# Attention prepared two chunks ahead, narrow sums in column halves, and one stream of weight conversions, in an attention and mixture-of-experts kernel

## The chip, the core and the metric

One core of a Trainium2 chip. The metric is the device time of one execution in microseconds; lower is better. Engines: PE (TensorE, matrix products), DVE (VectorE), ACT (ScalarE), POOL (GpSimd), and SP, which here issues the transfers between memory and the core's SBUF. PE writes its results into PSUM, eight banks of 512 columns of fp32; DVE and ACT read them there.

## What is computed

The reference has three stages, one after the other, over 4 batches of 768 tokens, 3072 in all:

```python
for t in range(S):                                  # attention, 8 heads of 48
    cur = einsum('bhd,bhe->bhde', u * k[t], v[t])
    y[t] = einsum('bhd,bhde->bhe', r[t], state + cur)
    state = w[..., None] * state + einsum('bhd,bhe->bhde', k[t], v[t])
x = y                                               # 3072 x 384
h = x @ w_in                                        # first MLP, 384 -> 2048 -> 384
x = (maximum(h, 0) + alpha * minimum(h, 0)) @ w_out
logits = x @ w_gate                                 # second: 8 experts, 384 tokens each
for e in range(8):                                  # greedy assignment by logit
    out[mask[e]] = maximum(x[mask[e]] @ w1[e], 0) @ w2[e]
```

The first MLP's weights arrive as 8-byte numbers and are converted on the core.

## The kernel before, in words

**Attention** runs over 24 chunks of 128 tokens (6 per batch, the four batches in turn). Within a chunk the recurrence is written as matrix products: r and k are scaled by powers of w (RT, KT), pA = K R^T for all pairs of tokens, a mask keeps the earlier tokens, the diagonal gets the sums cs of r u k, and y is the sum of the masked product with v and of the carried state SW with r. State products kv are added to SW (L401) and scaled (L382), for all chunks but the last four, which are the ends of the four batches.

The order of the work on each engine is the order in which the program is written. A *turn* (`turn`, L347) works on chunk i and ends chunk i-1, and prepares chunk i+1. It is a generator with three yields; after each part the main loop (L1256) lets one call of the weight stream pass, four a turn, from turn 2 on. The parts:

1. PE: diagonal sums cc of chunk i, four products of 128 columns by 2 (L360), which the trace counts as eight passes; DVE copies them to cs (L363). DVE: two predicated copies of pA into AT of chunk i-1 (L366). PE: state times r into y (SW, L371). PE: transposes of the scaled k of chunk i+1 into pk (L327). POOL: scaling of k for chunk i+2 (L312). ACT: four scalings of the identity by cs into AT (L378), KT from pk (L333). DVE: RT of chunk i+1 (L319). POOL: scaling of the state (L382).
2. PE: state products kv of chunk i (L389), in alternating column halves; PE: AT times v into y (L396), halves too. DVE: two additions Sn of kv (L401). ACT: four more scalings into AT (L404).
3. POOL: product of RT and KT of chunk i+1 (L339), from which the next turn's cc is made. ACT: ysb from y (L409); SP stores it in `xd`.
4. PE: pA of chunk i (L423), in row halves.

After a turn SP issues the loads of chunk i+4 (L1258). `warm` (L249) issues products without use.

**The weight stream** `load_weights` (L459) goes over 32 pieces, 16 of `w_in` and 16 of `w_out`. For each it issues a load some pieces ahead, and `weight_split` (L435) converts one: ACT makes mk (L443), DVE makes ti in three steps (L446, L448, L450) and tf in a fourth (L453), ACT casts tf to the high part (L456) and POOL subtracts for the low part (L457). It yields after each DVE step and after the last two operations, so a piece is five calls. Pieces 0 to 15 are converted in attention, with ti in PSUM; a second stream converts pieces 16 to 31 in the first group of the MLP, with ti in SBUF, five calls per column block.

**The first MLP** (`mlp`, L569) has seven groups of tokens (512, ..., 256). For each of 16 column blocks f: nine products of layer 1 (L649), ACT and DVE make gh and gl (L653 to L673), and twelve products of layer 2 two blocks behind (L599), for which piece f of `w_out` must be converted. In the second group DVE makes the gate's columns (`gate_columns`, L511) from `wgb`, whose buffer takes the converters' place (L616 to L618). Then come routing and the experts, which the change doesn't touch.

## Time and profile before

| what | us |
|---|---|
| median of 3 runs (lowest, highest) | 846.56 (845.14, 846.89) |
| the profiled execution | 845.94 |
| its span, first to last instruction | 843.9 |
| busy: PE, DVE, ACT, POOL | 801.2, 573.7, 407.8, 283.6 |

The profile is one execution. Busy is the time in which an engine had an instruction running; an engine that isn't busy waits, and the trace says for which instruction of which engine. PE's clock is granted by the chip: 1.00 stands for 2.4 GHz, 0.50 for 1.2 GHz. Attention fills about the first 157 us, the first MLP's first group the next 86.

### The profile page before, as it was taken

To read this page: it belongs to the slowest core of one execution; us is meant where nothing else is said; L and a number is where in the kernel's file an instruction comes from. 1 tells how busy PE (TensorE), PEld (TensorE's weight loads), DVE (VectorE), ACT (ScalarE), POOL (GpSimd) and SP (SyncE) were. 2 spreads that over 40 slices of the span, in tenths; PEclk is the share of its full clock that TensorE was granted. 3 is DMA by queue.
4 is the path that set the end of the run, shared out by engine and by line. 5 is a ranking of instruction groups with operands and counts; after the bars stand their busy time and mean duration, and the time that the engine had idled before them with its cause. 6 is when DMAs were issued, how large, how long until landed. Compare 5 with 4: busy or idle time off the path is not lost.

```text
span 843.9 us, 16328 instructions
## 1 busy us (share of the span) xinstructions
PE 801.2 (95%) x5955; PEld 734.0 (87%) x5955; DVE 573.7 (68%) x1535; ACT 407.8 (48%) x875; POOL 283.6 (34%) x268
## 2 busy tenths in 40 slices
PE   7899899899989999999999999997799999999996
PEld 6788788688879999999999999987799899899996
DVE  4777776589969998998988534576766666664221
ACT  2777676656544444453444445651444343344441
POOL 5566675322200000000000000002576766668661
PEclk8899898999999999999999999999899999999998
DMA  5676754242140020021002001004525523535400
GB/s 164 180 205 192 201 175 137 85 131 90 60 150 1 1 75 1 1 72 51 28 20 75 1 1 57 19 1 142 184 75 184 193 87 135 191 107 181 141 29 31
DMA packets 64584, 81.37 MB, mean 96 GB/s; under 512 B 8048, under 2 KB 55408, under 8 KB 64368
## 3 DMA queue, kind: packets, MB, share of 16 engines
q1 hardware_dynamic: 61008, 70.81, 27.1%
q0 software_dynamic: 3072, 9.44, 3.2%
q8 instruction: 49, 0.80, 0.4%
q14 instruction: 39, 0.32, 0.1%
q10 hardware_dynamic: 416, 0.00, 0.0%
HBM read 66.07 MB, written 14.16 MB: 95 GB/s over the span
## 4 chain that ended last, share of the span: by engine, by line
PE 66%; DVE 6%; issue 4%; ACT 2%; POOL 2%; DMA 1%; POOLq 0%; ACTq 0%; DVEq 0%
PE m L599 23%; PE ph L649 20%; PE eph L1099 10%; PE o L1116 9%; PE cnt L789 2%; PE ept L1083 1%; DMA wgb<-in_moe_w_gate_dram 1%; ACT nt L653 1%; DVE gh L662 1%; DVE gt L662 1%; POOL out_dram L1125 1%; POOL wbl L1063 1%; DVE G L784 0%; ACT wbh L456 0%; PE ip L878 0%
## 5 line engine op out<-in xcount | busy, mean ns | idle before, releaser
L649 PE MATMUL ph<-xh,wah 128*128 128x512 f32 (+1 forms) x336 | 122.6, 365 | 0.3 <-ACT gh L654 0.2
L649 PE MATMUL ph<-xl,wah 128*128 128x512 f32 (+1 forms) x336 | 122.4, 364 | 0.3 <-DVE xl L507 0.3
L649 PE MATMUL ph<-xh,wal 128*128 128x512 f32 (+1 forms) x336 | 122.1, 364 | 0.0
L599 PE MATMUL m<-wbh,gl 128*128 128x384 f32 (+1 forms) x352 | 119.4, 339 | 2.5 <-DVE gl L673 2.5
L599 PE MATMUL m<-wbh,gh 128*128 128x384 f32 (+1 forms) x352 | 119.5, 340 | 2.3 <-ACT wbh L456 2.3
L599 PE MATMUL m<-wbl,gh 128*128 128x384 f32 (+1 forms) x352 | 120.4, 342 | 1.3 <-POOL wbl L457 1.3
L653 ACT ACTIVATE nt<-ph 128x512 f32<-128x512 f32 (+1 forms) x112 | 60.2, 537 | 111.2 <-PE ph L649 103.0
L739 POOL COPY L<-M 128x176 f32<-128x176 f32 (+1 forms) x2 | 0.7, 358 | 332.5 <-DVE M L605 311.5
L670 ACT CAST gh<-gt 128x512 fp32r<-128x512 f32 (+1 forms) x96 | 56.3, 587 | 89.4 <-DVE gt L662 89.4
L662 DVE SCALAR_TENSOR_TENSOR gt<-nt,al,gt 128x512 f32<-128x512 f32 (+1 forms) x96 | 67.7, 705 | 45.0 <-ACT gt L654 44.5
L1107 DVE SCALAR_TENSOR_TENSOR hl<-eph,hh 128x384 fp32r<-128x384 f32 x64 | 35.6, 556 | 77.0 <-ACT hh L1102 77.0
L1102 ACT ACTIVATE hh<-eph 128x384 fp32r<-128x384 f32 x64 | 31.5, 492 | 114.5 <-PE eph L1099 111.8
L521 DVE SCALAR_TENSOR_TENSOR junk<-wt,wgb 128x384 f32<-128x384 f32 x128 | 71.3, 557 | 9.1 <-DMA wgb<-in_moe_w_gate_dram 5.2
L599 PEld LDWEIGHTS m<-wbl,gh 128*128 128x128 f32 x352 | 66.2, 188 | 7.7 <-POOL wbl L457 4.4
L649 PEld LDWEIGHTS ph<-xh,wal 128*128 128x128 f32 x336 | 63.4, 189 | 10.9
L599 PEld LDWEIGHTS m<-wbh,gh 128*128 128x128 f32 x352 | 66.2, 188 | 6.2 <-ACT wbh L456 2.7
L649 PEld LDWEIGHTS ph<-xh,wah 128*128 128x128 f32 x336 | 63.4, 189 | 8.6 <-ACT gh L654 0.5
L649 PEld LDWEIGHTS ph<-xl,wah 128*128 128x128 f32 x336 | 63.5, 189 | 8.3 <-DVE xl L507 0.6
L673 DVE TENSOR_TENSOR gl<-gt,gh 128x512 fp32r<-128x512 f32 (+1 forms) x96 | 61.6, 642 | 12.0 <-ACT gh L670 11.9
L1063 POOL TENSOR_TENSOR wal<-raw,wah 128x768 fp32r<-128x768 f32 x32 | 58.4, 1845 | 32.9 <-ACT wah L1062 31.4
L1063 POOL TENSOR_TENSOR wbl<-raw,wbh 128x768 fp32r<-128x768 f32 x32 | 58.6, 1849 | 30.4 <-ACT wbh L1062 30.3
L599 PEld LDWEIGHTS m<-wbh,gl 128*128 128x128 f32 x352 | 66.3, 188 | 2.9 <-DVE gl L673 2.9
(251 smaller groups left out, 1833.6 us busy)
## 6 DMA issues: line engine op xcount, KB each, us to landing
raw<-in_moe_w_dram SPq DMA_DIRECT2D x64, 384.0 KB, 4.7
stg<-in_moe_w_in_dram SPq DMA_DIRECT2D x16, 384.0 KB, 4.4
stg<-in_moe_w_out_dram SPq DMA_DIRECT2D x16, 384.0 KB, 3.1
raw_r<-in_rt_dram SPq DMA_DIRECT2D x24, 224.0 KB, 4.2
raw_k<-in_kc_dram SPq DMA_DIRECT2D x24, 192.0 KB, 4.0
raw_v<-in_vc_dram SPq DMA_DIRECT2D x24, 192.0 KB, 4.2
xd<-ysb SPq DMA_DIRECT2D x48, 96.0 KB, 2.2
md<-raw SPq DMA_DIRECT2D x22, 192.0 KB, 2.0
```

Of the source, the lines that this page charges most:

```text
L521: v.scalar_tensor_tensor(junk, t, 1.0, self.wgb[:, e], op0=ALU.mult, op1=ALU.mult, accum_out=wc[:, f, e:e + 1])
L599: nc.tensor.matmul(acc[t][:, :N], a[:, o], self.wb[b][:, f, :N], start=(f == 0 and n == 0), stop=(f == NF - 1 and n == 2))
L649: nc.tensor.matmul(ph[:, :T], self.wa[a][:, k, fs], b[:, k, :T], start=(n == 0), stop=(n == 8))
L653: nc.scalar.activation(nt[:, :T], ph[:, :T], AF.Relu, scale=-1.0)
L662: v.scalar_tensor_tensor(gt[:, :T], nt[:, :T], self.al[:, f:f + 1], gt[:, :T], op0=ALU.mult, op1=ALU.add)
L670: nc.scalar.copy(h, g)
L673: v.tensor_sub(l, g, h.bitcast(F32))
L1063: self.nc.gpsimd.tensor_sub(to[1], d, to[0].bitcast(F32))
L1099: self.nc.tensor.matmul(ph, w1[a][:, k, f * P:(f + 1) * P], x[b][:, k], start=(n == 0), stop=(n == 8))
L1102: self.nc.scalar.activation(hh, ph, AF.Relu)
L1107: self.nc.vector.scalar_tensor_tensor(hl, ph, 0.0, hh.bitcast(F32), op0=ALU.max, op1=ALU.subtract)
L1116: self.nc.tensor.matmul(self.acc[q], h[a][:, o], w2[b][:, f], start=(f == 0 and n == 0), stop=(f == NS - 1 and n == 2))
```

## The change

Attention prepares chunk i+2 in turn i (LOOK) and needs the deeper buffers for that. The sums of chunk i+1 are made in part 2 of turn i (`sums`), ahead of kv, in eight products of 64 columns; they lie in the last eight columns of the tile that also takes kv (`kvc`). The two weight streams become one, whose loads use the buffers `raw`; what attention doesn't get to is converted in the first MLP group. Four chunks and three weight pieces are loaded ahead of the set-up's branch.

```diff
-EARLY = 16
-WAHEAD = 2
-EARLYC = 2
+WAHEAD = 3
+EARLYC = 4
-NRAW = {"k": 4, "r": 4, "v": 6, "p": 3}
-AHEAD = 4
+NRAW = {"k": 4, "r": 4, "v": 6, "p": 5}
+AHEAD = 5
+LOOK = 2
...
-        self.load_chunk(0)
+        for i in range(EARLYC):
+            self.load_chunk(i)
+            if i:
+                next(self.wl)
...
+        self.kvc = self.pa.tile([P, 4 * D + H], F32, tag="kv", name="kvc")
...
+    def sums(self, i):
+        if i >= NCH:
+            return
+        cc, prod = self.kvc[:, 4 * D:], self.prod.pop(i)
+        for j in range(4):
+            for c in range(2):
+                o = slice(64 * c, 64 * c + 64)
+                self.nc.tensor.matmul(cc[o, 2 * j:2 * j + 2], prod[:, j, o], self.uw[:, j, :], start=True, stop=True,
+                                      skip_group_check=True)
+        cs = self.cs[i] = self.wk.tile([P, H], F32, name="cs")
+        self.nc.vector.tensor_copy(cs, cc)
...
-        RT = self.RT[i] = self.wk.tile([112, 4, P], F32, name="RT", bufs=3)
+        RT = self.RT[i] = self.wk.tile([112, 4, P], F32, name="RT", bufs=4)
...
-        KT = self.KT[i] = self.wk.tile([112, 4, P], F32, name="KT")
+        KT = self.KT[i] = self.wk.tile([112, 4, P], F32, name="KT", bufs=3)
...
-            cc = self.pa.tile([P, H], F32, tag="cc", name="cc")
-            prod = self.prod.pop(i)
-            for j in range(4):
-                nc.tensor.matmul(cc[:, 2 * j:2 * j + 2], prod[:, j, :], self.uw[:, j, :], start=True, stop=True,
-                                 skip_group_check=True)
-            cs = self.wk.tile([P, H], F32, name="cs")
-            v.tensor_copy(cs, cc)
+            cs = self.cs.pop(i)
...
-            y = self.pa.tile([112, 4, P], F32, tag="y", name="y")
+            y = self.pa.tile([112, 4, P], F32, tag="y", bufs=2, name="y")
...
-        self.turn_k(i + 1)
-        self.scale_k(i + 2)
+        self.turn_k(i + LOOK)
+        self.scale_k(i + LOOK + 1)
         if cur:
-            AT = self.AT[i] = self.wk.tile([P, 2, 4, P], F32, name="AT", bufs=3)
+            AT = self.AT[i] = self.wk.tile([P, 2, 4, P], F32, name="AT", bufs=2)
...
-        self.keep_k(i + 1)
-        self.scale_r(i + 1)
+        self.keep_k(i + LOOK)
+        self.scale_r(i + LOOK)
...
         yield
+        self.sums(i + 1)
         kv = None
         if cur and c < NCB - 1:
-            kv = self.pa.tile([112, 4, D], F32, tag="kv", name="kv")
+            kv = self.kvc[:112, :4 * D].rearrange("p (j d) -> p j d", j=4)
...
-        self.product(i + 1)
+        self.product(i + LOOK)
...
     def weight_load(self, shape, src):
+        t = self.rw.tile([P, 2 * DM], F32, name="raw")
...
             ti = (self.pa.tile([P, n], U32, tag="ti", name="ti") if self.pa is not None else
-                  self.stg.tile([P, n], U32, name="ti", bufs=1))
+                  self.pc.tile([P, n], U32, tag="cnt", name="ti"))
...
-        side = self.load_weights(EARLY, 2 * NF)
+        side = self.wl
...
+        K.rw = ctx.enter_context(tc.tile_pool(name="rw", bufs=4, reuse_waits="tile"))
+        wl = K.wl = K.load_weights(WAHEAD)
         K.att_setup(c2)
-        wl = K.load_weights(0, EARLY, WAHEAD)
-        K.scale_k(0, tc.nc.vector)
-        K.scale_k(1)
-        K.prepare(0)
-        drain(cut(wl, WAHEAD))
+        v = tc.nc.vector
+        for i in range(LOOK + 1):
+            K.scale_k(i, None if i else v)
+        for i in range(LOOK):
+            K.scale_r(i)
+            K.turn_k(i)
+            K.keep_k(i)
+            K.product(i, None if i else v)
+        K.sums(0)
+        for i in range(EARLYC, AHEAD):
+            K.load_chunk(i)
         for i in range(NCH + 1):
             merge((K.turn(i), 1), (cut(wl, PACE) if i > 1 else None, 1))
             K.load_chunk(i + AHEAD)
...
-        drain(wl)
+        while K.splitting:
+            next(wl)
         K.warm(4)
```

The product, ysb and set-up tiles get three buffers in the same way. The pool `stg` keeps only the converters' own tiles.

## Rows read from the trace of the kernel before

**Rows 1.** The page: busy time, share of the span and instructions of PE, PEld, DVE, ACT, POOL.

```profile
PE 801.2 (95%) x5955; PEld 734.0 (87%) x5955; DVE 573.7 (68%) x1535; ACT 407.8 (48%) x875; POOL 283.6 (34%) x268
```

**Rows 2.** Table by stretch: us, busy PE, PEld, DVE, ACT, POOL, clock, DMA share, GB/s.

```profile
34.00:130.00 96.00, 88.60 (x1082) 79.32 (x1080) 69.99 (x149) 68.04 (x188) 62.45 (x61) 0.89 0.68 196
...
157.00:243.00 86.00, 79.51 (x373) 67.31 (x373) 69.20 (x119) 49.12 (x96) 18.77 (x16) 0.98 0.37 118
```

**Rows 3.** Timeline of PE in one turn: start, us, engine, line, operation, idle before.

```profile
81.21 1.16 PE L423 MATMUL pA<-RT,KT 48*128 48x128 f32 x16
82.30 1.05 PE L360 MATMUL cc<-uw,prod 112*128 112x2 f32 x8
83.21 1.11 PE L371 MATMUL y<-RT,SW 112*112 112x128 f32 x8
...
84.69 0.61 PE L389 MATMUL kv<-raw_v,raw_p 128*64 128x48 f32 x15
...
85.13 0.22 PE L389 MATMUL kv<-raw_v,raw_p 128*64 128x48 f32 x1
...
86.17 1.16 PE L423 MATMUL pA<-RT,KT 48*128 48x128 f32 x16
```

**Rows 4.** Timeline of PE: pA of chunk 3 and of chunk 19.

```profile
33.31 1.16 PE L423 MATMUL pA<-RT,KT 48*128 48x128 f32 x16
...
129.49 1.16 PE L423 MATMUL pA<-RT,KT 48*128 48x128 f32 x16
```

**Rows 5.** List of waits, 13 to 157 us: waiter, releaser, total us, times, longest.

```profile
PE cc L360 <- POOL prod L339: 12.3, 13, 2.0
```

**Rows 6.** Two waits of cc (timeline of PE), and the clock after them (table by stretch).

```profile
72.37 1.05 PE L360 MATMUL cc<-uw,prod 112*128 112x2 f32 x8 [0.48 <-POOL prod L339]
...
93.46 1.05 PE L360 MATMUL cc<-uw,prod 112*128 112x2 f32 x8 [0.89 <-POOL prod L339]
...
71.20:74.50 3.30, 2.82 (x33) 2.63 (x30) 1.04 (x3) 1.29 (x4) 2.10 (x3) 1.00 0.47 112
...
95.00:98.40 3.40, 3.40 (x36) 3.06 (x35) 2.54 (x6) 2.64 (x9) 0.94 (x1) 0.50 0.68 206
```

**Rows 7.** Timeline of DVE in one turn.

```profile
115.61 1.35 DVE L366 COPY_PREDICATED AT<-later,pA 128x512 f32<-128x512 int32 x2
...
117.45 0.55 DVE L446 TENSOR_SCALAR ti<-stg 128x384 uint32<-128x384 uint32 x1
117.90 0.71 DVE L401 TENSOR_TENSOR Sn<-kv,SW 48x192 f32<-48x192 f32 x2
118.65 0.56 DVE L448 SCALAR_TENSOR_TENSOR ti<-stg,ti 128x384 uint32<-128x384 uint32 x1
...
119.91 0.55 DVE L453 SCALAR_TENSOR_TENSOR tf<-mk,ti 128x384 f32<-128x384 f32 x1
```

**Rows 8.** Timeline of DVE, ACT and PE where attention ends and the MLP begins.

```profile
154.46 1.34 DVE L366 COPY_PREDICATED AT<-later,pA 128x512 f32<-128x512 int32 x2 [2.32 <-PE pA L423]
...
157.50 1.66 ACT L506 CAST xh<-xr 128x512 fp32r<-128x512 f32 x3
...
158.17 0.49 PE L649 MATMUL ph<-xh,wah 128*128 128x512 f32 x1
```

**Rows 9.** The chain of waits in the first MLP group and the start of the second.

```profile
161.17 0.60 ACT nt L653
...
168.79 2.87 PE m L599 x11
...
233.65 6.26 DMA wgb<-in_moe_w_gate_dram
...
247.14 2.08 PE m L599 x12
...
251.32 2.09 PE m L599 x12
```

**Rows 10.** Groups by line, DVE, 160 to 235 us: busy, mean ns, idle before.

```profile
L453 DVE SCALAR_TENSOR_TENSOR tf<-mk,ti 128x384 f32<-128x384 f32 x16 | 17.5, 1094 | 2.5 <-ACT mk L443 2.3
```

More of the change, by code (lines that the diff above doesn't have):

```diff
@@ L169, in att_setup @@
                 self.raw[n, i] = t
-        self.load_chunk(0)
+        for i in range(EARLYC):
+            self.load_chunk(i)
+            if i:
+                next(self.wl)
         self.wk = ctx.enter_context(tc.tile_pool(name="wk", bufs=2))
-        self.stg = ctx.enter_context(tc.tile_pool(name="stg", bufs=WAHEAD + 1))
-        TR = ap.tile([112, 4, P], F32, name="TR")
-        TK = ap.tile([112, 4, P], F32, name="TK")
+        self.stg = ctx.enter_context(tc.tile_pool(name="stg", bufs=2))
+        TR = self.wk.tile([112, 4, P], F32, tag="ysb", bufs=3, name="TR")
+        TK = self.wk.tile([112, 4, P], F32, tag="prod", bufs=3, name="TK")
         PW = ap.tile([112, 8, 4], F32, name="PW")
@@ L216, in att_setup @@
         self.WC = PW[:, 7, :].unsqueeze(2).to_broadcast([112, 4, 112])
-        self.AT, self.prod, self.RT, self.KT = {}, {}, {}, {}
-        for i in range(1, EARLYC):
-            self.load_chunk(i)
+        self.AT, self.prod, self.RT, self.KT, self.cs = {}, {}, {}, {}, {}
+        self.kvc = self.pa.tile([P, 4 * D + H], F32, tag="kv", name="kvc")
         self.branch(fl)
-        for i in range(EARLYC, AHEAD):
-            self.load_chunk(i)
         self.warm(WARM[2])
@@ L244, in range_test @@
         v.tensor_copy(ok, oki)
-        po = self.pa.tile([1, 4], F32, tag="cc", name="pok")
+        po = self.pa.tile([1, 4], F32, tag="y", bufs=2, name="pok")
         nc.tensor.matmul(po, self.ones[:112], ok, start=True, stop=True)
@@ L260, in recurrence @@
         TB = 4
-        St = self.wk.tile([P, 12, D], F32, tag="AT", bufs=3, name="slow_s")
+        St = self.wk.tile([P, 12, D], F32, tag="AT", bufs=2, name="slow_s")
         v.memset(St, 0.0)
@@ L270, in recurrence @@
         with tc.For_i(0, S, TB) as t0:
-            rk = self.wk.tile([P, 2, TB, 12], F32, tag="prod", name="slow_rk")
-            vt = self.wk.tile([P, TB, D], F32, tag="AT", bufs=3, name="slow_v")
+            rk = self.wk.tile([P, 2, TB, 12], F32, tag="prod", bufs=3, name="slow_rk")
+            vt = self.wk.tile([P, TB, D], F32, tag="AT", bufs=2, name="slow_v")
             for bh in range(B * H):
@@ L279, in recurrence @@
                     nc.sync.dma_start(vt[4 * bh + g:4 * bh + g + 1], self.v[b, h:h + 1, bass.ds(t0, TB), :])
[L280 removed]
+            py = self.pa.tile([D, TB, 32], F32, tag="y", bufs=2, name="slow_py")
             for t in range(TB):
                 sh = [P, 12, D]
[L283 removed]
+                kv = self.wk.tile(sh, F32, tag="RT", bufs=4, name="slow_kv")
                 v.tensor_tensor(kv, rk[:, 1, t].unsqueeze(2).to_broadcast(sh),
                                 vt[:, t].unsqueeze(1).to_broadcast(sh), op=ALU.mult)
[L286 removed]
+                z = self.wk.tile(sh, F32, tag="KT", bufs=3, name="slow_z")
                 v.tensor_tensor(z, kv, wu[:, 1].unsqueeze(2).to_broadcast(sh), op=ALU.mult)
@@ L289, in recurrence @@
                 v.tensor_tensor(z, z, rk[:, 0, t].unsqueeze(2).to_broadcast(sh), op=ALU.mult)
-                yp = self.wk.tile([P, D], F32, tag="ysb", name="slow_yp")
+                yp = self.wk.tile([P, D], F32, tag="ysb", bufs=3, name="slow_yp")
                 v.tensor_reduce(yp, z.rearrange("p j e -> p e j"), axis=AX, op=ALU.add)
@@ L331, in keep_k, with product @@
             return
-        KT = self.KT[i] = self.wk.tile([112, 4, P], F32, name="KT")
+        KT = self.KT[i] = self.wk.tile([112, 4, P], F32, name="KT", bufs=3)
         self.nc.scalar.copy(KT, self.pk)
-    def product(self, i):
+    def product(self, i, g=None):
         if i >= NCH:
             return
-        t = self.prod[i] = self.wk.tile([112, 4, P], F32, name="prod")
-        self.nc.gpsimd.tensor_mul(t, self.RT[i], self.KT[i])
-    def prepare(self, i):
-        self.scale_r(i)
-        self.turn_k(i)
-        self.keep_k(i)
-        self.product(i)
+        t = self.prod[i] = self.wk.tile([112, 4, P], F32, name="prod", bufs=3)
+        (g or self.nc.gpsimd).tensor_mul(t, self.RT[i], self.KT[i])
     def turn(self, i):
@@ L405, in turn @@
         yield
-        self.product(i + 1)
+        self.product(i + LOOK)
         if prev:
-            ysb = self.wk.tile([112, 4, P], F32, name="ysb")
+            ysb = self.wk.tile([112, 4, P], F32, name="ysb", bufs=3)
             nc.scalar.copy(ysb, y)
@@ L426, in weight_load @@
     def weight_load(self, shape, src):
+        t = self.rw.tile([P, 2 * DM], F32, name="raw")
+        n = shape[1] * shape[2]
         if src.dtype == F32:
-            t = self.stg.tile(shape, F32, tag="stg", name="stg")
+            t = t[:, :n].rearrange("p (a b) -> p a b", a=shape[1])
             self.nc.sync.dma_start(t, src)
         else:
-            t = self.stg.tile([P, shape[1] * shape[2], 2], U32, tag="stg", name="stg")
+            t = t.bitcast(U32)[:, :2 * n].rearrange("p (n w) -> p n w", w=2)
             self.nc.sync.dma_start(t.rearrange("p (a b) w -> p a (b w)", a=shape[1]), src)
@@ L457, in weight_split, with load_weights @@
         nc.gpsimd.tensor_sub(dst_l, t, dst_h.bitcast(F32))
-    def load_weights(self, n0, n1, ahead=1):
+    def load_weights(self, ahead):
+        n0, n1 = 0, 2 * NF
+        self.split_done = 0
         d = 2 if self.w_in.dtype != F32 else 1
```

9 lines of the change are left out of this document (4 added, 5 removed).

## The prediction

> **What bounds the kernel now.** I read the page first: TensorE (PE) is busy for 95% of the span [rows 1], so what counts is where PE waits or runs at half rate. A table by stretch comes next: in the attention turns from 34 to 130 us PE is 88.6 of 96 us busy, but at a mean granted clock of 0.89; its two levels are 2.4 and 1.2 GHz, so some 22% of that stretch, 21 us, ran at 1.2 [rows 2]. Then the timeline of one clean turn: from one pA to the next 4.96 us, of which the diagonal sums cc take 0.91 (82.30 to 83.21), SW and pk 1.48, kv 0.44 (84.69 to its last matmul at 85.13), y 1.04, pA 1.09 [rows 3]. Yet the sixteen turns from pA of chunk 3 to pA of chunk 19 take 96.2 us, 6.01 each [rows 4]. The list of waits names the first cause: cc waits for POOL's product, 13 times, 12.3 us [rows 5]. The product needs KT, KT comes on ScalarE (ACT) behind four AT scalings, and those need the cs of the turn before: a ring through four engines about as long as a turn. The second cause follows from it. Where the wait was 0.48 (cc at 72.37) the clock stayed at 1.00; where it was 0.89 (cc at 93.46), with 0.91 of narrow cc behind it, the next 3.4 us were granted 0.50 [rows 6].
>
> VectorE (DVE) is the engine next in line. Per turn: the two predicated copies and RT 1.84 (115.61 to 117.45), a conversion step 0.45 to 0.63 (117.45 to 117.90; two from 118.65 to 119.91 in 1.26), 0.58 taken, Sn 0.75 [rows 7].
>
> **The change, part by part.** *Looking two chunks ahead.* KT, RT and the product are made a turn earlier, and cs too, so the ring is cut: cc no longer waits for POOL, and the AT scalings no longer wait for cs. POOL has the same four operations as before with a turn more of slack, and the deeper buffers (RT, KT, product, ysb, y) cover it. The second y bank frees PE from the ysb copy, which no row shows as a wait. AT goes from three buffers to two: AT(i) then needs y of turn i-1 finished, which ACT waits for anyway with its ysb copy just ahead; nothing. Chunk loads are issued five ahead instead of four but are used a chunk earlier, so SP has the same lead.
>
> *Sums in column halves.* Eight passes of 128 columns become sixteen of 64. The kv row is the like of it: sixteen passes of 64 and 48 columns in alternating halves, 0.44 [rows 3]. I take 0.44 between 0.40 and 0.91 (halves one after the other). A clean turn of PE becomes 4.96 - 0.91 + 0.44 = 4.49. The Trainium skill (TensorE: Matmul & The Clock Gate, Part 3, "What overlaps and what doesn't") says that a weight load overlaps running matmuls only where the row group differs; the halves share all rows, so by it the sums would stay at 0.91. The kv row speaks against that, its halves sharing all rows too; by the rule the sum below would be some 2 us higher, in the four last turns.
>
> *The shared bank: a new wait.* cc and kv now lie in one tile. Program order is: PE writes the sums, DVE copies them to cs, PE writes kv, DVE adds Sn. Every PSUM tile of the kernel before fills a bank of its own and goes strictly from all of PE's writes to the reader, so no row shows PE writing one part of a tile while DVE reads another. Either the wait is by address (kv does not wait, cost 0) or for the whole bank (kv waits for cs). I take the bank, nearest to the strict alternation of kv and Sn now. The Trainium skill (PSUM — Partial Sum Buffer, "PSUM bank collisions raise a hardware error") has this as its rule, guard by bank and not by address; no row here shows it.
>
> With that wait PE holds kv, and behind it y and pA, until DVE reaches cs. DVE in the turn: copies and RT 1.84, one conversion step 0.58, cs 0.17; a hand-over 0.1 (ACT's first cast ends 0.12 before the first MLP matmul [rows 8]); PE then kv, y, pA 2.57; hand-over 0.1: 5.36 from pair of copies to pair of copies. DVE itself: 1.84 + 0.58 + 0.17 + 0.7 until kv has landed + Sn 0.75 + three steps 1.74 = 5.78. The stream has five calls a piece, four with a DVE step, and four calls a turn; so in five turns one has all four steps (5.8), three miss one behind Sn (5.4), one misses the one ahead of cs (about 5.2): mean 5.45. PE stands 0.96 a turn, 1.3 in the long one.
> Sixteen turns: 16 x (5.45 - 6.01) = **-9.0**. Turns 2 and 3, which ran clean before, go from 4.96 to 5.45: **+1.0**.
>
> *Clock in attention.* Wait and narrow sums together are now 0.96 + 0.44 = 1.40 in most turns, like 0.48 + 0.91 = 1.39 at 72 us, where the clock stayed; in the long turn 1.35 + 0.44 = 1.79, like 0.89 + 0.91 = 1.80 at 93 us, where it fell [rows 6]. One turn in five of sixteen is three falls, at half rate for 3.4 us each, 1.7 lost: **+5**. Ends: 0, and one in every other turn, +14.
>
> *The last four chunks* have no kv, so nothing waits for cs. PE: 4.49 - 0.44, say 4.1 a turn; 16.4, plus pA and hand-over 1.3 to the last pair of copies: 17.7. Before, from 129.49 to 154.46, 24.97 with a wait and a half-rate stretch [rows 4, 8]: **-7.3**. DVE needs 3.8 there.
>
> *One stream of conversions.* Three of its calls lie in the set-up; 92 calls in 23 turns and three more convert 19 pieces before the MLP, 16 before this. The three more lie in turns 21 to 24, which have room on DVE, but five steps stand behind the last pair of copies: 1.24 + 5 x 0.58 = 4.15, and a cast of 0.5 on ACT, ahead of the first xh cast, which came 3.04 after the copies began (154.46 to 157.50) [rows 8]: **+1.5**. Three weight loads are now queued on SP among the first chunks; SP issues, it doesn't compute, and the first pA waits for POOL's second product, so I book nothing, with 2 us either way.
> In the first MLP group the first layer-2 batch waited for its converted weights until 168.79, and batch 17 starts at 247.14; the batches then follow each other in 4.18 (247.14 to 251.32) [rows 9]. After: pieces 0 to 2 of w_out are ready, so batch 0 starts after three layer-1 batches (158.17 to 161.17, then twice 2.1) and 0.4 for gl: 165.8. DVE then has 13 groups with five calls, and its last conversion step takes 1.09 there with both inputs in SBUF [rows 10] against 0.55 in attention with one in PSUM [rows 7]; with ti moved to PSUM a group needs 0.67 + 2.4 + 0.65 = 3.7 of DVE, under PE's 4.18. The stream ends three groups earlier, so wgb, whose buffer waits for the converters' space and which held the chain for 6.26 us [rows 9], lands in time. Batch 17 at 165.8 + 17 x 4.18 = 236.9: **-10.2**. From there PE is the bound as before.
>
> Sum: +1.0 - 9.0 + 5 - 7.3 + 1.5 - 10.2 = -19.0. The profiled execution took 845.94 (span 843.9, 2.0 around it); 845.9 - 19.0 = 826.9, and the median of the runs stands 0.6 above the profiled one: **827**.
>
> **Rivals.** *No bank wait.* If kv waits by address, a turn is the larger of PE's 4.49 and DVE's 1.84 + 0.1 + 0.75 + 3.2 x 0.58 = 4.55; say 4.6 with jitter: 16 x (4.6 - 6.01) = -22.6, the early turns -1, no falls. -1 - 22.6 - 7.3 + 1.5 - 10.2 = -39.6: 807. For it: the sums and kv touch different columns of the tile. Against: the strict alternation in every bank now. Chance 0.12.
> *The MLP keeps its pace.* If DVE still sets the first group's pace, or wgb still comes late, the gain is only the first wait: from 168.79 to 165.8 and what was lost to a half-rate stretch after it, some 5 of the 10.2: 832. For it: DVE is 69 of 86 us busy there now [rows 2]; against: the 3.7 above. Chance 0.10.
> *Slower: the new wait brings the clock down.* It stands in each of the 16 turns, between sums and kv, and both neighbours are narrow. If most turns fall to half rate as at 93 us, each costs 1.7; the other terms are worth 24, so it decides from the fourteenth fall on. Sixteen: 846.5 - 24 + 27 = 849.5. For it: a wait of 0.89 was enough once; against: the cc that stood behind it is halved. Chance 0.05.
> *The change doesn't do what it says*: product(i) might still be late, as POOL's scaling waits for raw_k. Two turns of lead cover that; I give it none.
>
> **How the numbers follow.** Forecast 0.73, at 827, its own range 816 to 839 (clock 0 to +14, turn length 0.2 x 16, start 2). About a tenth, all of the address case, lies below 811, and a tenth above 839 with the clock. So 811 to 839. A measurement of this kernel tells 0.2%, 1.7 us, from no change. Faster 0.94, same 0.01, slower 0.05.
>
> **What would show it.** Right: PE's wait for POOL's product gone; a wait of kv for DVE's cs in turns 1 to 19 with 0.8 to 1.3 each; pA to pA 5.4; sums in 0.44; layer-2 batch 0 right behind the third layer-1 batch; no DVE wait for wgb; xh later behind the last copies by 1.5. Wrong: kv straight behind the sums (then 807), a clock under 0.85 from 34 to 125 us, or batches of the first group at 4.3 and more.

## The result, and the profile after

The changed kernel takes 836.03 us (median of 7 runs, 834.65 to 841.36); the kernel before, on the same chip, 846.56. The ratio is 0.9888, with a 95% interval of 0.9862 to 0.9914: faster by 1.1%, and inside the range, but by 10.5 us where 19.5 were forecast. The profiled execution took 834.65, its span is 832.9 us, 11.0 less than before. These 11.0 fall on the stretches of the sum as follows:

| stretch | forecast, us | measured, us |
|---|---|---|
| start to pA of chunk 3 (33.31, now 38.19) | +1.0 | +4.9 |
| sixteen turns to pA of chunk 19 (96.18, now 86.73) | -9.0, and +5 for the clock | -9.5 |
| to pA of chunk 23 (23.71, now 15.42), forecast to the copies behind it | -7.3 | -8.3 |
| to the first ph (4.97, now 6.63) | +1.5 | +1.7 |
| first ph to layer-2 batch 17 (88.97, now 89.05) | -10.2 | +0.1 |

The page of the changed kernel, busy time by engine, as [rows 1]:

```profile
PE 785.5 (94%) x6147; PEld 717.9 (86%) x6147; DVE 576.9 (69%) x1536; ACT 406.7 (49%) x875; POOL 280.2 (34%) x269
```

The table by stretch, with the columns of [rows 2]; the first line is exactly the sixteen turns:

```profile
38.20:124.90 86.70, 74.34 (x1209) 65.56 (x1208) 70.83 (x149) 66.97 (x185) 61.94 (x61) 1.00 0.74 215
147.00:236.00 89.00, 82.98 (x385) 69.79 (x386) 69.99 (x124) 47.38 (x92) 19.52 (x22) 0.98 0.29 93
```

The clock of the turns went from 0.89 to 1.00, and PE is now idle for 12 of 86.7 us: it was slow, now it waits. What for, the list of waits from 13 to 157 us says, which had POOL's product at this place [rows 5]:

```profile
PE kvc L390 <- DVE cs L318: 15.3, 20, 2.0
```

One turn on PE, as [rows 3]. From pA to pA it is 5.25 to 5.33; every fifth takes 5.85; the mean of the sixteen is 86.73 / 16 = 5.42, for which 5.45 was forecast:

```profile
70.96 1.16 PE L424 MATMUL pA<-RT,KT 48*128 48x128 f32 x16
72.06 1.13 PE L371 MATMUL y<-RT,SW 112*112 112x128 f32 x8
73.02 0.60 PE L339 MATMUL pk<-ident,raw_p 128*112 128x128 f32 x4
73.55 0.63 PE L315 MATMUL kvc<-uw,prod 112*64 112x2 f32 x16
74.75 0.61 PE L390 MATMUL kvc<-raw_v,raw_p 128*64 128x48 f32 x15 [0.56 <-DVE cs L318]
...
76.23 1.16 PE L424 MATMUL pA<-RT,KT 48*128 48x128 f32 x16
```

The sums and kv write different columns of one tile, and kv stands 0.56 us for the copy cs. Why the copy is late, DVE's timeline shows: a conversion step stands ahead of it, and Sn behind it then waits 0.84 for kv.

```profile
74.07 0.56 DVE L453 SCALAR_TENSOR_TENSOR ti<-raw,ti 128x384 uint32<-128x384 uint32 x1
74.53 0.16 DVE L318 COPY cs<-kvc 128x8 f32<-128x8 f32 x1
75.53 0.72 DVE L402 TENSOR_TENSOR Sn<-kvc,SW 48x192 f32<-48x192 f32 x2 [0.84 <-PE kvc L390]
```

Where the first MLP group begins, the timelines of POOL and DVE show something new. POOL's memsets of a routing constant, which ran from 150.1 to 155.4 beside the end of attention before, now run beside the group's start, and two small DVE instructions take over 4 us; the first gt waits behind them:

```profile
148.12 5.24 POOL L139 MEMSET ohr<- 128x3072 bf16 x2
...
149.15 4.30 DVE L120 TENSOR_SCALAR tri<-jp 128x128 bf16<-128x128 int32 x1
149.28 4.18 DVE L133 TENSOR_SCALAR io<-io 128x32 f32<-128x32 f32 x1
...
153.82 0.74 DVE L669 SCALAR_TENSOR_TENSOR gt<-nt,al,gt 128x512 f32<-128x512 f32 x1
```

Within the group, ACT and DVE in one column block:

```profile
166.22 0.51 ACT L459 CAST wbh<-tf 128x384 fp32r<-128x384 f32 x1 [1.28 <-DVE tf L456]
166.64 0.59 ACT L660 ACTIVATE nt<-ph 128x512 f32<-128x512 f32 x1
167.13 0.59 ACT L661 ACTIVATE gt<-ph 128x512 f32<-128x512 f32 x1
...
165.63 0.55 DVE L456 SCALAR_TENSOR_TENSOR tf<-mk,ti 128x384 f32<-128x384 f32 x1
166.10 0.69 DVE L680 TENSOR_TENSOR gl<-gt,gh 128x512 fp32r<-128x512 f32 x1
167.75 0.75 DVE L669 SCALAR_TENSOR_TENSOR gt<-nt,al,gt 128x512 f32<-128x512 f32 x1 [0.96 <-ACT gt L661]
```

Read it as a ring. The stream's five calls now fill one block exactly, so a piece's cast (its fifth call) is the last thing that ACT is given in a block, and it waits for tf, the fourth DVE step. The next block's nt and gt stand behind that cast, though ph has long been there, and DVE's L669 waits 0.96 us for gt. DVE goes idle for the very engine that waits for DVE. The block takes 4.67 us (163.08, 167.75, 172.42), where PE needs 4.2. At 4.3 and more the prediction had called itself wrong. In the kernel before the stream's first call in this group was a load alone, and the cast fell behind gh of the following block.

At the start, ACT's first AT scaling was at 14.98 before; now it waits for SP, which leaves the branch (L229, around the recurrence, whose tiles share AT's buffers) only at 18.5:

```profile
18.57 1.28 ACT L378 ACTIVATE AT<-ident,cs 128x128 f32<-128x128 f32 x4 [4.80 <-SPq L229]
```

### The profile page after: what moved, and what is told of

It is laid out like the page before. It is cut to its first block, busy times and chain, and to the rows that moved or that the text cites. A ratio compares the mean times of both kernels' runs of the same rounds, so it can differ in the third digit from the quotient of the medians.

```text
span 832.9 us, 16734 instructions
## 1 busy us (share of the span) xinstructions
PE 785.5 (94%) x6147; PEld 717.9 (86%) x6147; DVE 576.9 (69%) x1536; ACT 406.7 (49%) x875; POOL 280.2 (34%) x269
## 3 DMA queue, kind: packets, MB, share of 16 engines
q1 hardware_dynamic: 61008, 70.81, 27.5%
## 4 chain that ended last, share of the span: by engine, by line
PE 69%; DVE 15%; issue 6%; ACT 4%; POOL 2%; DMA 1%; DVEq 0%; POOLq 0%; SPq 0%; ACTq 0%
PE m L605 21%; PE ph L656 19%; PE eph L1106 10%; PE o L1123 9%; PE cnt L796 2%; DVE AT L366 2%; DVE ti L451 2%; DVE ti L449 2%; PE y L397 2%; PE kvc L390 1%; DVE ti L453 1%; DVE tf L456 1%; PE pA L424 1%; DVE RT L331 1%; ACT nt L660 1%
## 5 line engine op out<-in xcount | busy, mean ns | idle before, releaser
L669 DVE SCALAR_TENSOR_TENSOR gt<-nt,al,gt 128x512 f32<-128x512 f32 (+1 forms) x96 | 67.8, 706 | 52.7 <-ACT gt L661 52.7
L1114 DVE SCALAR_TENSOR_TENSOR hl<-eph,hh 128x384 fp32r<-128x384 f32 x64 | 35.6, 557 | 77.4 <-ACT hh L1109 77.4
```

The costliest lines, as they stand in the source:

```text
L669: v.scalar_tensor_tensor(gt[:, :T], nt[:, :T], self.al[:, f:f + 1], gt[:, :T], op0=ALU.mult, op1=ALU.add)
L1114: self.nc.vector.scalar_tensor_tensor(hl, ph, 0.0, hh.bitcast(F32), op0=ALU.max, op1=ALU.subtract)
```

## The experiments

Each is an edit of the changed kernel and computes all of it. What stands against the kernel before is a ratio. The chips differ: in five groups of runs the kernel before took 846.4, 845.7, 855.8, 852.2 and 846.0 us. Its start also varies from run to run. So most readings are by stage, from one trace of each:

| kernel | ratio (95%) | pA of chunk 3 | 16 turns | to first ph | first ph to the group's stores | rest |
|---|---|---|---|---|---|---|
| before | 1 | 33.3 | 96.2 | 28.7 | 79.3 | 606.4 |
| changed | 0.989 (0.986, 0.991) | 38.2 | 86.7 | 22.0 | 82.2 | 603.7 |
| e1_phase | 0.981 (0.978, 0.984) | 38.5 | 86.7 | 22.0 | 75.1 | 604.0 |
| e2_consts | 0.989 (0.986, 0.992) | 40.8 | 90.4 | 22.4 | 80.5 | 604.2 |
| e3_loads | 0.987 (0.984, 0.990) | 35.7 | 86.7 | 22.0 | 82.2 | 603.6 |
| e4_sums_first | 0.995 (0.992, 0.997) | 36.2 | 88.3 | 27.6 | 82.3 | 603.6 |
| e5_full | 0.992 (0.988, 0.995) | 39.1 | 86.7 | 23.0 | 82.3 | 603.6 |
| e6_warm | 0.990 (0.985, 0.994) | 37.0 | 90.9 | 22.0 | 82.2 | 603.7 |
| e8_sums_before_step | 0.987 (0.983, 0.992) | 36.6 | 83.8 | 22.4 | 82.3 | 603.6 |
| e9_sums_mid | 0.977 (0.971, 0.982) | 35.6 | 78.8 | 25.6 | 82.2 | 611.4 |
| e10_mid_prod | 0.975 (0.972, 0.978) | 34.9 | 76.4 | 22.9 | 82.2 | 603.8 |
| e11_prod_up | 0.988 (0.982, 0.994) | 37.5 | 90.8 | 22.0 | 82.3 | 610.3 |
| e12_phase_mid | 0.964 (0.960, 0.968) | 36.1 | 76.4 | 22.9 | 75.2 | 611.5 |
| e14_all | 0.964 (0.960, 0.969) | 37.1 | 77.3 | 22.9 | 72.6 | 611.1 |
| e15_loads_warm | 0.984 (0.980, 0.989) | 38.2 | 89.1 | 22.0 | 82.2 | 608.1 |
| e16_all_warm | 0.962 (0.959, 0.965) | 36.0 | 76.7 | 22.9 | 72.6 | 609.5 |
| e17_chunks | 0.990 (0.985, 0.995) | 38.8 | 86.7 | 22.0 | 82.3 | 608.8 |
| e18_chunk4_first | 0.986 (0.982, 0.990) | 33.8 | 86.7 | 22.0 | 82.2 | 603.8 |
| e19_all_chunk4 | 0.960 (0.957, 0.964) | 31.6 | 78.0 | 22.9 | 74.1 | 603.6 |

The second column from the right is the first MLP group up to the store of its results, 6.8 us before batch 17 in the changed kernel. In the kernel before the group lost more behind its stores, at the wait for wgb. The last column shows which rows share a chip's pace: the only edited thing in it is the routing constants, which four of the kernels make there, and e2_consts shows no more than 0.2 us for them (604.2 against the 604.0 of e1_phase on the same chip).

### The first MLP group

**e1_phase** shifts the stream by one call:

```diff
-                drain(cut(side, rate))
+                drain(cut(side, rate - (gi == 0 and f == 0)))
```

> The stream of weight conversions is drained with four steps instead of five in the first block of the first MLP group and with five from then on, as in the kernel before, so that a piece's cast on ACT comes after the next block's gh and no longer stands, waiting for DVE's tf, ahead of the next block's nt and gt. Theory (the ring of ACT and DVE through the aligned stream holds the group): the block period falls from 4.67 to 4.2 to 4.4 us, DVE's waits of 0.96 for ACT's gt go from most blocks, the m batch that stood at 236.0 comes 4 to 6 us earlier, the whole 830 to 832 us. Rival 1 (DVE's own work, some 4.2 us in a block, and PE's half clock at the group's start hold it): under 1 us, 835 to 836. Rival 2 (the last pieces of w_out are now late for layer two or the gate columns, as one step is left over): 837 or more.

Measured 828.44 us, less than the 830 to 832 expected; the group is 7.1 us shorter, attention unchanged. ACT and DVE after the shift:

```profile
166.16 0.51 ACT L459 CAST wbh<-tf 128x384 fp32r<-128x384 f32 x1
166.57 0.55 ACT L446 ACTIVATE mk<-raw 128x384 f32<-128x384 f32 x1
167.02 0.58 ACT L660 ACTIVATE nt<-ph 128x512 f32<-128x512 f32 x1
...
167.87 0.69 DVE L680 TENSOR_TENSOR gl<-gt,gh 128x512 fp32r<-128x512 f32 x1
168.47 0.75 DVE L669 SCALAR_TENSOR_TENSOR gt<-nt,al,gt 128x512 f32<-128x512 f32 x1
169.13 0.55 DVE L449 TENSOR_SCALAR ti<-raw 128x384 uint32<-128x384 uint32 x1
```

No wait stands in brackets any more: the cast follows gh, and L669 follows gl at once. DVE's block is 3.62 us (164.85, 168.47, 172.09), as the prediction had worked out 3.7, and PE sets the pace. In the chain of waits batches alternate with layer 1 without a gap from the first on, where the chain of the changed kernel had run through ACT and DVE until batch 12 at 215.1:

```profile
157.79 2.02 PE m L605 x10
159.81 2.10 PE ph L656 x9
161.91 2.08 PE m L605 x12
...
229.15 2.12 PE m L605 x12
```

From first ph (147.22) to batch 17 (229.15) it is 81.9 instead of 89.05, where the prediction's terms give 78.8 (88.97 less 10.2). The ring is shown; it cost 7.1 us.

**e2_consts** moves `route_consts` from the start of the first group to block 2 of the second.

> The routing constants (GpSimd's two memsets of 2.65 us and iotas, VectorE's five small instructions) are made in block 2 of the second group instead of at the start of the first. Theory (the memsets run beside VectorE's first steps of the group and stretch its two small instructions from about 0.2 to 4.2 us): the first gt comes 1 to 1.5 us earlier than 153.8, the whole 834.5 to 835. Rival 1 (those instructions overlap work that waits for the first ph anyway, and the stream sets the pace): within 0.4 us of the changed kernel. Rival 2 (in the second group the same instructions stretch too, and layer one waits there): slower by 1 to 3 us.

The group is 1.7 us shorter, and L120 took 0.22 us at its new place. The whole, at 837.11, shows nothing: in this trace the half clock held until 50 us, and the first ph came 6.6 us later. So the effect is read from the stage. With the shifted stream, e14_all takes 72.6 there against 75.2 in e12_phase_mid, 2.5 us less, but not all of that is the constants: e12_phase_mid has a half clock at the group's start (136.5 to 139.8), e14_all has 1.00 throughout. e19_all_chunk4, also without the constants, has a half clock of about that length (134.0 to 137.4) and takes 74.1. So, from one trace of each, 1.1 us of the 2.5 go with the constants and 1.4 with the clock; whether the memsets have a part in the clock is open, since e2_consts has the half clock without them. The changed kernel has it too (147.1 to 150.4). From first ph to batch 17 the steps are 89.05, 81.9 without the ring, 80.9 without the constants too (e19_all_chunk4), and 79.5 without the half clock (e14_all), close to the 78.8 of the prediction.

### The turn

**e8_sums_before_step** issues the sums before the turn's first yield, so that DVE's copy no longer stands behind a conversion:

```diff
+        self.sums(i + 1)
         yield
-        self.sums(i + 1)
```

> The sums and their copy are issued ahead of the turn's first conversion step instead of behind it; TensorE's order stays as it is, only VectorE's copy now comes before the conversion. Theory (kv waits 0.56 us because the copy stands behind a conversion of 0.56, the bank itself costs no more than the copy's way, 0.2 us): kv waits 0.2 us, turns 4.9 to 5.1 instead of 5.27, the long ones 5.5, the whole 830 to 833 us. Rival 1 (VectorE's work sets the turn): turns 5.2 to 5.3, the whole 835 to 836.5. Rival 2 (with shorter turns GpSimd's product comes late for the sums and the clock falls in every fifth turn): long turns of 7 us or more, the whole 836 or more.

By stage, as the theory had it: kv waits 0.27 in the clean turns, which take 4.97; of every five, one takes 5.32 and one 5.38; the sixteen take 83.8 us, of which one early turn of 6.63 holds a half clock (40.5 to 43.8). The whole, 833.97 us, is not clear of the changed kernel: the intervals of the ratios overlap.

```profile
72.64 0.61 PE L390 MATMUL kvc<-raw_v,raw_p 128*64 128x48 f32 x15 [0.27 <-DVE cs L318]
74.13 1.16 PE L424 MATMUL pA<-RT,KT 48*128 48x128 f32 x16
```

**e4_sums_first** goes further: sums at the top of the turn, the copy between the two predicated copies.

```diff
             for q in range(2):
                 v.copy_predicated(...)
+                if q == 0:
+                    self.sums(i + 1)
```

> The sums of the next chunk stand at the top of a turn on TensorE, ahead of the state products and the transposes, and their copy on VectorE between the two predicated copies instead of behind the conversions, so that the products into the bank that sums and kv share come long after the copy. Theory (the wait of 0.56 to 1.1 us for the copy, and VectorE's 0.84 for kv behind it, set the turn): a turn falls from 5.42 to about 4.8 us (then ACT's 4.8 us of work in a turn and TensorE's 4.7 set it), 20 turns, the whole 823 to 827 us. Rival 1 (the work of VectorE and ACT sets the turn, the wait fills a gap): turns 5.2 to 5.4, the whole 832 to 836. Rival 2 (the second predicated copy and the AT behind it are now late for y): turns 5.5 or more, the whole 838 or more.

A miss. The clean turns are 4.63, and yet the whole is 840.78: one turn in five takes long, three of them 8.3 to 9.7. PE's timeline and the table by stretch there:

```profile
66.78 1.16 PE L427 MATMUL pA<-RT,KT 48*128 48x128 f32 x16
69.97 1.02 PE L315 MATMUL kvc<-uw,prod 112*64 112x2 f32 x16 [2.03 <-POOL prod L351]
...
72.00:74.00 2.00, 2.00 (x14) 1.66 (x15) 0.95 (x2) 0.08 (x1) 0.93 (x1) 0.50 0.90 309
```

This is the picture of the kernel before [rows 5, 6]: sums at the top of a turn meet a product that isn't ready, and the half clock follows. POOL's product stood behind the weight subtraction, which waits for ACT's cast:

```profile
67.70 1.00 POOL L463 TENSOR_TENSOR wal<-tf,wah 128x384 fp32r<-128x384 f32 x1 [1.75 <-ACT wah L462]
68.66 1.26 POOL L351 TENSOR_TENSOR prod<-RT,KT 112x512 f32<-112x512 f32 x1
```

**e10_mid_prod** puts the sums between state products and transposes and issues the product at the end of part 1, ahead of that subtraction:

```diff
+        self.sums(i + 1)
         self.turn_k(i + LOOK)
...
+        self.product(i + LOOK)
         yield
-        self.sums(i + 1)
...
-        self.product(i + LOOK)
```

> The sums stand between the state products and the transposes, their copy on VectorE behind the predicated copies, and GpSimd's product two chunks ahead is issued at the end of the turn's first part, ahead of a weight subtraction that it stood behind in some turns. Theory (the copy and kv no longer wait, as the experiment with the sums first showed with clean turns of 4.63; that one lost its gain to a wait of 2.03 us for GpSimd's product in every fifth turn, behind which the clock fell; here the product comes before the subtraction): clean turns 4.6 to 4.8, the long ones under 5.6, no half clock between 40 and 140 us, the whole 822 to 828 us. Rival 1 (another engine, ACT with 4.8 us of work in a turn or GpSimd with 4.2, makes TensorE wait all the same, and the clock falls again): long turns of 7 us or more, the whole 834 to 842.

Measured 824.53 us, with every turn from chunk 3 to chunk 19 at 4.77 to 4.79. PE is busy 75.01 of 76 us at full clock:

```profile
35.00:111.00 76.00, 75.01 (x1205) 65.36 (x1207) 71.08 (x147) 64.82 (x183) 62.42 (x62) 1.00 0.83 242
```

**e9_sums_mid** and **e11_prod_up** each make one half of this edit.

> Half of the edit that gave turns of 4.78: the sums stand between the state products and the transposes, but GpSimd's product stays in the turn's third part, behind the weight subtraction in some turns. Theory (the sums then come before the late product: in the experiment with the sums first the wait was 2.03 us, here 1.1 us of state products lie ahead of them): in every fifth turn TensorE waits 0.5 to 1.2 us for the product, and the half clock comes back, long turns of 6 to 9 us, the whole 830 to 840 us. Rival (the place of the sums alone gives the gain): turns of 4.8 throughout, the whole 822 to 827.

> The other half: GpSimd's product is issued at the end of the turn's first part, the sums stay at the changed kernel's place. Theory (kv still waits for the copy behind a conversion): turns 5.27, the long ones 5.3 to 5.85, the whole 832 to 836 us. Rival (the late product sets the changed kernel's turn too): turns of 5 us or less, the whole 823 to 830.

In the sixteen turns the sums' place brings most of it (78.8), with a wait of 0.97 for the product in every fifth, which then takes 5.82. The half clock that was expected behind that wait came once in three: behind the waits at 67.74 and 92.67 the clock stayed at 1.00, behind the third, in the turn after chunk 19, it fell.

```profile
117.62 0.63 PE L315 MATMUL kvc<-uw,prod 112*64 112x2 f32 x16 [0.98 <-POOL prod L351]
...
119.00:121.50 2.50, 2.50 (x24) 2.17 (x23) 1.65 (x4) 2.41 (x7) 1.68 (x2) 0.50 0.57 205
```

So from pA of chunk 3 to the first ph (108.8 us in the changed kernel, 104.4 here, 99.4 in e10_mid_prod) the sums' place brings 4.4 us and the product's place behind it another 5.0. The product's place alone brings nothing to the clean turns (5.25 to 5.32); its 90.8 holds a half clock in the first turns (43.2 to 53.4).

**e5_full** makes the sums with four full-width products again.

```diff
-            for c in range(2):
-                o = slice(64 * c, 64 * c + 64)
-                self.nc.tensor.matmul(cc[o, 2 * j:2 * j + 2], prod[:, j, o], self.uw[:, j, :], start=True, stop=True,
+            self.nc.tensor.matmul(cc[:, 2 * j:2 * j + 2], prod[:, j, :], self.uw[:, j, :], start=True, stop=True,
```

> The sums are made by four products of 128 columns of the array instead of eight of 64 (as in the kernel before, but into the shared bank and at the changed kernel's place). Theory (the halves save what the two rows show, 1.05 for the eight full products of both trace groups against 0.63 for sixteen halves, some 0.4 us in a turn, and it all lies ahead of the copy that kv waits for): turns 5.27 to 5.5 to 5.7, the last four 3.6 to 4.0, the whole 841 to 846 us. Rival 1 (the copy stands behind a conversion on VectorE anyway, which ends 0.35 us after the sums): turns 5.3 to 5.4, the last four 0.4 longer, the whole 837 to 840. Rival 2 (the width of the products changes nothing): within 1 us.

Rival 1 came: the sums take 0.32 more and the wait behind them 0.22 less.

```profile
74.42 0.95 PE L313 MATMUL kvc<-uw,prod 112*128 112x2 f32 x8
75.71 0.61 PE L388 MATMUL kvc<-raw_v,raw_p 128*64 128x48 f32 x15 [0.34 <-DVE cs L316]
77.20 1.16 PE L422 MATMUL pA<-RT,KT 48*128 48x128 f32 x16
```

The turn is 5.28 against 5.27. Only where nothing waits for the copy do the halves show: from chunk 19 on, turns of 4.39, 4.40, 3.95 and 3.60 against 4.08, 4.07, 3.68 and 3.59. The column halves are worth 0.9 us in all, in these traces.

### The start

Five kernels, in the order of the expectations below. **e3_loads**: the three early weight loads behind the branch. **e6_warm**: six idle products of the identity behind each of the first two transposes. **e15_loads_warm**: these two together. **e17_chunks**: chunks 2 and 3 and the weight loads behind the branch, no idle products. **e18_chunk4_first**: as e15_loads_warm, with chunk 4 ahead of the weights, which is the edit shown:

```diff
         for i in range(EARLYC):
             self.load_chunk(i)
-            if i:
-                next(self.wl)
...
+            K.warm(6)
             K.product(i, None if i else v)
...
         for i in range(EARLYC, AHEAD):
             K.load_chunk(i)
+        drain(cut(wl, WAHEAD))
```

> The three early weight loads are issued behind the branch instead of between the chunk loads ahead of it; chunks 0 to 3 stay ahead of it. Theory (SyncE comes out of the branch late, at 18.5, because of the loads that are queued ahead of it, and ACT's first scaling waits 4.8 us for SyncE's place in the program): SyncE's next load comes at 14 to 15, the first scaling at 14 to 15.5, the pA of turn 3 at 34 to 36.5 instead of 38.2, the whole 832 to 834.5. Rival 1 (the half clock of TensorE from 14 to 27.7 alone makes the start long): the scaling earlier, the pA of turn 3 within 1 us of 38.2, the whole 835 to 836. Rival 2 (chunks are enough to hold SyncE): neither moves by over 1 us.

> Six more idle products of the identity on TensorE behind each of the first two chunks' transposes in the set-up. Theory (the half clock from 14 to 27.7 us comes of TensorE's gaps at 10.9 to 14, and is what costs the start its 4.9 us): full clock until 20 at least, the pA of turn 3 at 34.5 to 36.5 instead of 38.2, the whole 832 to 834.5. Rival 1 (the clock falls all the same, later or as before, since the scaling that waits for SyncE until 18.5 leaves TensorE idle): the pA of turn 3 at 38 to 40, the whole 835.5 to 838.

> The weight loads behind the branch and the idle products in the set-up, both, on the changed kernel. Alone, the first brought the scaling from 18.6 to 15.0 and the pA of turn 3 from 38.2 to 35.7 with a half clock from 18 to 24.5 and 28.5 to 32; the second held the full clock until 22.5, but the scaling stood at 18.4, and the pA of turn 3 came at 37.0. Theory (two causes that each hold the start: SyncE late out of the branch, and the clock): the scaling at 15 to 15.5, the pA of turn 3 at 32.5 to 34.5, as in the kernel before (33.3), 4 to 5 us less than the changed kernel up to there. Rival (the clock falls later for as long, whatever goes before it): the pA of turn 3 at 35 to 37, and no gain over the loads alone.

> Chunks 2 and 3 and the weights are all loaded behind the branch, as in the kernel before; chunks 0 and 1 ahead of it. Theory (SyncE's time out of the branch follows what is queued ahead of it): SyncE's next load at 12.5 to 13.5, the first scaling at 14 to 14.5, but chunk 2's k then lands after 17 and GpSimd's scaling of it, with its transposes, waits: the pA of turn 3 at 35 to 38. Rival (the branch takes until 15 whatever is queued): the scaling at 15 or later.

> As the run with the loads behind the branch and the idle products, but chunk 4 is now loaded ahead of the three weight loads, right behind the branch. There, the clock stayed full until 26.5 and turn 1 took 4.77, and then GpSimd's scaling waited 4.91 us for chunk 4's k, TensorE 1.5 and 1.5 us, and the half clock from 26.5 to 47 followed. Theory (the start was held by three waits in a row, each of which brought the clock down: SyncE's late way out, TensorE's gaps, chunk 4 behind the weights): GpSimd's scaling of chunk 4 at 19.5 to 21, no half clock before 30, the pA of turn 3 at 32 to 34.5, some 4 to 5 us before the changed kernel's 38.2. Rival (the clock falls in these turns whatever the waits): the pA of turn 3 at 35 or later.

| kernel | first AT scaling, us | half clock between 9 and 40 us | pA of chunk 3 |
|---|---|---|---|
| before | 14.98 | 16.5 to 23.3, from 37 | 33.31 |
| changed | 18.57 | 14.0 to 27.5, 31 to 34.5 | 38.19 |
| e3_loads | 15.02 | 18 to 25, 28.5 to 32 | 35.72 |
| e6_warm | 18.40 | 22.5 to 25.5, 29 to 32.5 | 37.01 |
| e17_chunks | 14.05 | 14 to 27.5, 31 to 34 | 38.84 |
| e15_loads_warm | 15.85 | from 26.5 to 47 | 38.15 |
| e18_chunk4_first | 15.69 | 26.5 to 29.5 | 33.79 |

SP leaves the branch the later, the more is queued ahead of it: at 13.1 with chunks 0 and 1, 14.9 to 15.8 with four chunks, 18.4 to 19.1 with weights too. The loads alone brought the scaling forward and left a half clock of 10 us; the idle products alone put the half clock off and left the scaling where it was. In e17_chunks the scaling came first of all, at 14.05, but the half clock was as long as in the changed kernel, and so was the start. With the loads and the idle products together, turn 1 ran at full speed (4.77), but the edit had put chunk 4 behind the weights, and a half clock of 20 us followed that wait. The same late chunk stands in e3_loads, where POOL's scaling of it waited 5.71 us, so that run has two causes in it. POOL's scaling of chunk 4, in e15_loads_warm and then in e18_chunk4_first:

```profile
23.85 1.00 POOL L323 TENSOR_TENSOR raw_p<-raw_k,TKm 128x384 f32<-128x384 f32 x1 [4.91 <-DMA raw_k<-in_kc_dram]
```

```profile
18.74 1.01 POOL L322 TENSOR_TENSOR raw_p<-raw_k,TKm 128x384 f32<-128x384 f32 x1
```

With that wait gone the start is 0.5 us off that of the kernel before, though a half clock of 3 us came all the same. So the 4.9 us went with SP's late way out of the branch and with the half clock in the first turns; an earlier way out without idle products gave 2.5 us back in e3_loads and nothing in e17_chunks, where chunks 2 and 3 come later too. It is one trace each, and the start of one and the same set-up varies by 2 us or more, so the share of each stays open, and the whole time of e18_chunk4_first, 831.75 us, is not clear of the changed kernel (0.986 and 0.989, overlapping intervals). What SP waits for inside the branch no view shows.

### Together

**e12_phase_mid**: the stream's shift of e1_phase and the turn of e10_mid_prod.

> Both gains together: the shifted stream in the first MLP group (measured at 828.4 alone) and the sums in the middle with the product early (824.5 alone). If they are independent: 817 us, and the first group's batches stand 4 to 7 us earlier against the first ph than with the sums alone. If the stream's place in the first group was already changed by the shorter attention, under half of the 7 us adds: 821 to 824.

**e14_all**: these, with the loads of e3_loads and the constants of e2_consts.

> As the run before, with the weight loads behind the branch and the routing constants in the second group. Theory: the pA of turn 3 1 to 3 us earlier, the first group 1 to 1.7 us shorter, the whole 2.5 to 4.5 us below the run before, some 813 to 815 us. Rival (the start varies by as much by its clock from run to run, and the earlier scaling is given back there): within 1.7 us of the run before.

**e16_all_warm**: these, with the idle products of e6_warm.

> All the edits that shortened their stretch: the shifted stream, the sums in the middle with the early product, the weight loads behind the branch, the routing constants in the second group, and the idle products in the set-up. Theory (each edit acts in its own stretch): the pA of turn 3 at 32 to 34, turns of 4.8, the first group 72.6 to 73 us from the first ph to its stores, the whole 811 to 815 us on a chip where the kernel before takes 846. Rival (the clock gives the start back later in the first turns): 815 to 819.

**e19_all_chunk4**: these, with the loads in the order of e18_chunk4_first.

> The same order of loads in the kernel with all the edits. Theory: the pA of turn 3 at 31 to 33.5 instead of 36.0, the whole 3 to 4 us below the version before it, whose ratio to the kernel before was 0.962, so 0.958. Rival: 0.961 or more.

The gains of the stream's shift and of the turn add up (75.2 and 76.4 us, each as alone): e12_phase_mid took 825.00 us where the kernel before took 855.8, a ratio of 0.964, which would be 816 us at the 846.5 of the result, an estimate. In e14_all the group's 2.5 us came, the start's did not (37.1), as its rival said, and the ratio stayed where it was. e16_all_warm still had chunk 4 behind the weights; its start, 36.0, missed the forecast of 32 to 34, while its ratio of 0.962 lies within the 811 to 815 of 846. e19_all_chunk4 takes **811.53 us** (811.02 to 812.84) where the kernel before takes 845.98: 0.9602 (0.9568, 0.9636). It beats both kernels. Its start came as forecast (31.6), but the sixteen turns and the group each took over 1 us more than in e16_all_warm, both with a half clock that e16_all_warm does not have there (35.0 to 38.4, 134.0 to 137.4). The interval of its ratio holds the 0.958 of the theory and the 0.961 of the rival, so the whole time does not decide between them.

## Why the prediction was right and wrong

**The step that failed is the term of the first MLP group, -10.2, measured +0.1.** It counted DVE's work per block, 3.7 us under PE's 4.18, and concluded that PE would set the pace. The 3.7 was right (3.62 in e1_phase), and so were the two things it rested on: L456 takes 0.55 with its input in PSUM, and wgb lands in time. What was left out is where the stream's calls fall in the orders of ACT and DVE. Merging two streams took away the odd first call, five calls then fitted one block exactly, and cast, nt and gt formed a ring with tf and L669. That cost 7.1 us. The rest lies at the group's start, where batch 0 came 10.6 us behind the first ph (146.97 to its first product with gl at 157.54) for the 7.6 forecast: the routing constants, 1.1 to 1.7 us, and a half clock, about 1.4, neither of which the term had. The prediction's rival "the MLP keeps its pace", at 832 with 0.10, had the place and half of the price, though not the mechanism: it looked for a DVE with too much work, and DVE stood idle 0.96 us in a block.

**The start, +1.0, measured +4.9.** "I book nothing" for the three weight loads on SP was the mistake: the prediction said that SP only issues, and did not ask what waits for SP. The AT scaling did, through a buffer shared with the branch's other path: its wait of 4.80 ends at SP's L229. The half clock of the first turns had no term either. The bound of 2 us either way was too small.

**The clock, +5, measured 0.** The term took wait plus narrow sums as what brings the clock down, 1.79 us in the long turn like 1.80 before (its own wait of 1.3 would have given 1.75). It rested on two of the 13 waits. The one of 0.48, said to leave the clock alone, stands right behind a stretch at 0.50 (68.0 to 71.0 us). And the trace of the kernel before holds a wait as long as the other, with the same cc behind it, that left the clock at 1.00 (timeline, and table by stretch):

```profile
125.61 1.05 PE L360 MATMUL cc<-uw,prod 112*128 112x2 f32 x8 [0.88 <-POOL prod L339]
...
126.00:132.00 6.00, 4.65 (x66) 4.11 (x66) 4.20 (x9) 4.36 (x12) 3.04 (x4) 1.00 0.89 267
```

In the changed kernel a wait of 1.14 with sums of 0.63 stands in every long turn and the clock stays at 1.00 for 86.7 us. In e2_consts, whose attention is the same, that wait left the clock alone twice (74.56, 101.52) and the third time did not:

```profile
128.49 0.97 PE L390 MATMUL kvc<-raw_v,raw_p 128*64 128x48 f32 x15 [1.14 <-DVE cs L318]
...
129.00:131.50 2.50, 2.50 (x29) 2.17 (x27) 1.73 (x4) 0.16 (x2) 2.38 (x3) 0.50 0.60 189
```

So the length of the single wait does not decide it; e9_sums_mid shows the same with 0.97. In e4_sums_first falls came behind waits of 0.26, 0.88 and 2.03 in three turns. What decides stays open. Without this term the turns would have been forecast at -9.0 against the -9.5 measured.

**Right:** that kv waits for cs, the gain in the last chunks (-8.3 for -7.3), and the later first ph (+1.7 for +1.5). The length of the turn came out too (5.42 for 5.45; the long turn 5.85 for 5.8), but in part by luck: PE's work was forecast at 4.49 with a wait of 0.96, and measured it is 4.71 (5.27 less 0.56) with a wait of 0.55 to 0.62, under the 0.8 to 1.3 that the prediction named as its sign. The two errors cancel. The Trainium skill (PSUM — Partial Sum Buffer, "PSUM bank collisions raise a hardware error") guards a bank and not an address; the 20 waits of kv agree with it, though they show the kernel's order and not what would happen without. From the Trainium skill's other rule (TensorE: Matmul & The Clock Gate, Part 3, "What overlaps and what doesn't"), that weight loads overlap running products only across row groups, the prediction had worked out sums of full length; here sixteen halves took 0.63 against 0.95 for eight full passes, so that length did not come. That does not refute the rule. The weight loads themselves were shorter, as PEld's timelines of the changed kernel and of e5_full show, and whether a load overlapped a running product these rows do not tell:

```profile
73.55 0.55 PEld L315 LDWEIGHTS kvc<-uw,prod 112*64 112x64 f32 x16 [0.17 <-issue]
...
74.31 0.97 PEld L313 LDWEIGHTS kvc<-uw,prod 112*128 112x128 f32 x8
```

The forecast of 0.44 was 0.1 too low: from the first sum to the next product it is 0.56 in e4_sums_first (77.59 to 78.15).

## What to carry to other kernels

Where a stream of side work is dealt out by calls, count not only the work of each engine but the place of each call in each engine's order: an operation that waits for another engine must not stand ahead of one that this other engine will need. When two tiles share a bank, put the reader of the first directly behind its writer, and the second writer late. Before work is put ahead of a branch or a wait on a queue that "only issues", look for every buffer that is released there. And before a rule read from two rows gets a price, hold it against every like row of the same trace.

## What had not been expected of the hardware

A DVE instruction that took 0.22 us elsewhere (L120 in e2_consts and in the kernel before) took 4.30 beside POOL's memsets and ended 0.1 us after them (153.45, 153.36). The predicated copies of the kernel before, 1.33 and 1.34 us for a pair beside the same memsets, took no longer than elsewhere. So only some instructions were held; which forms are, no run here tells. And the granted clock of the first 50 us differs between traces of the same set-up (pA of chunk 3 at 38.2, 38.5 and 40.8 in the changed kernel, e1_phase and e2_consts), so an edit there can't be judged by one time.
